# Sketched attention and a four-expert layer: keys issued ahead of the sketch matrices, pieces dealt to other slots, and a tail of 384 columns in two stores

## The chip, the cores and the metric

The kernel runs on one core of a Trainium2 chip. The metric is device time in microseconds (us). The core's engines have each their own instruction stream: TensorE (PE in the profile; PEld is its weight load), VectorE (DVE), ScalarE (ACT), GpSimd (POOL), and SyncE (SP), which here only issues DMAs. They wait for one another by semaphores. SBUF is the on-chip memory, PSUM the eight banks that TensorE writes its sums to.

## The reference

Attention with a quadratic feature map goes ahead of a weighted sum of four two-layer networks:

```python
def phi(x):                                   # 8 x 8 products of two sketches
    a = np.einsum('rd,bhsd->bhsr', S1, x)
    b = np.einsum('rd,bhsd->bhsr', S2, x)
    return np.einsum('bhsi,bhsj->bhsij', a, b).reshape(*x.shape[:-1], r * r)
q_p, k_p = (phi(q), phi(k))
kv = np.einsum('bhsf,bhsd->bhfd', k_p, v)
z = np.sum(k_p, axis=2)
num = np.einsum('bhsf,bhfd->bhsd', q_p, kv)
den = np.einsum('bhsf,bhf->bhs', q_p, z)[..., None] + 1e-06
...
x = attn_out.transpose(0, 2, 1, 3).reshape(B * S, H * D)      # 4352 tokens x 128
p = domain_probs / (domain_probs.sum(-1, keepdims=True) + 1e-09)
for e in range(E):
    h = np.maximum(x @ w1[e], 0.0)
    out += p[:, e:e + 1] * (h @ w2[e])
```

There are 4 batches, 4 heads, 1088 positions, 32 dimensions, sketches of rank 8; 4 experts of 1024 hidden units. All of it is float32. S1 and S2 come as 64-bit floats.

## The kernel before, in words

**Start.** ScalarE issues the load of S1 and SP that of S2, 8 rows each; then SP issues k of batch 0 (`load_k(0)`, 128 rows of 4352 B), the first q, v, and the weights. VectorE turns the 64-bit words of S1 and S2 into floats (`words`, L301 to L327); ScalarE and GpSimd lay them out as the weights sk, sp and sr (L336 to L343). Meanwhile TensorE runs 11 matmuls on constants (`keep_warm`, L275). VectorE transposes k (L424), and the first products k times sk (L287, the helper `on_side`) follow. L456 copies the products out of PSUM, L481 multiplies them into features.

**Columns.** The 4352 tokens are columns, cut into ten chunks: 128, 448, six of 512, 352, 352. For each chunk and each expert there are eight blocks of 128 hidden units. The list of *slots* is chunk by chunk, expert by expert, block by block; the host loop walks through it and writes out every engine's order by hand. One slot does, in this order: `opening` (first matmuls of block i), `second` (second-layer matmuls of block i - 5), `settle`, `third` (last first-layer matmul of earlier blocks, and what makes their parts), `pay` (late passes), and `work`, which deals pieces of attention.

**A block.** Float32 precision is had from fp32r matmuls by splitting operands in parts. First layer: L1068 and L1069 (wa by xa, wb by xb), then ScalarE scales the sum in its bank (L1070, factor 1 + 2^-12), and one slot later L1085 adds wd by xd. The result is split in three:

- ha, by ScalarE (L1103) or VectorE (L1107);
- hb = relu - ha, by VectorE (L1110), which also reads the bank;
- hc: a scaled part by ScalarE (L1105) or POOL (L1119, from ha), then POOL subtracts it from hb (L1120).

Which engine does what is a letter for each block, the *maker*: A has ha and the scaled part on ScalarE, P has ha on ScalarE and the scaled part on POOL, D has ha on VectorE and the scaled part on ScalarE, V makes hc on VectorE (L1112). X is a plain block: ScalarE's relu (L1095) of the whole sum, multiplied in one float32 pass. ha, hb and hc rotate through 5, 5 and 13 tiles; the tiles of hc also serve plain blocks and sums in order. A tile is free again once the matmul that reads it is done. Second layer: L1164 (va by ha) and L1165 (vb by hb) into one of two banks, in turn by expert, and the late passes L1199 (vd by hc, and the plain block), dealt by `DEALT` over the next expert's slots. Then `gather` multiplies by the expert's gate (L1302) and adds to the chunk's total (L1303), on VectorE; the bank is then free for the expert after the next. In chunk 0 the slots are pairs of blocks; the first two experts of chunk 1 are done in whole float32 (L1061, and L1148 for the second layer).

**Weights and tokens.** The parts of w1 (`weight_parts`; L846 scales on ScalarE or, in `split`, L848 on POOL; L851 joins on VectorE) and of w2 (va, vb, vd; L862) are made in slots listed in `W1_AT` and `W2_AT`. The tile of vd lies over the raw w2 and that of va over the raw w1. `token_parts` makes the three parts of a chunk (L851 on VectorE, then L915 on the engine that `XD_BY` names for that chunk).

**Attention in pieces.** `front` yields the attention of batches 1 to 3 as a stream of pieces: the keys of a batch (transposes L424; `key_project_wide`; L476 adds, the products L490 on VectorE, `value_copy` on the engine that `VALUES_BY` names, L434 to L439), and units of queries (transposes L594, products L783 on the engine that `Q_BY` names, stores L761 and re-loads through DRAM, `attend`). How fast pieces are dealt follows from `needed`, the count of pieces by which a chunk must be ready, plus `LEAD`; `FETCH` is the number of pieces between a unit's load and its product, `TOKENS_AT` the slot of chunk 1's token parts, `TURN` the slots between a chunk's last gather and its output transposes. Two clocks that add up what VectorE and ScalarE were given put pieces off, within limits.

**Tail.** The last expert of the last chunk has makers of its own, `MAKER_TAIL`. Its two Y blocks are relu times gate in one VectorE operation each (L1090), written with columns re-ordered by token. `gather_first` (L1291, L1292) gates and adds the early sums of that expert; its late passes go to another bank a (L1202), gated (L1234) and added into a column order by token (L1236). `last_rows` then multiplies the Y blocks with their weights so that tokens come out on partitions (L1247, three groups for 352 columns: 121, 121, 110 partitions) and adds the sums by a unit matrix (L1249); three copies (L1252 VectorE, L1254 ScalarE) and three stores (L1259: SP, ScalarE, and SP again) end the kernel. `ps_a` is one bank, `ps_h` five, `ps_o` two.

Of the kernel before, what the change touches and what calls it, by code (L numbers as in the profile page):

```python
# [24 lines left out]
def kernel(  # L25
# [39 lines left out]
    GE = 160  # L65
    LAG = 5
    GATES = 3
    BUFFERS = (5, 5, 13)
    HA, HB, HC = BUFFERS
    WHOLE = 2  # L70
    TURN = 3
    MAKER = 'VPXPAAAA'
    LATE = 2
    LATER = 99
    MAKER_1 = 'PPXPPDAP'
    MAKER_LATE = 'APXAPADA'
    TAIL = 4
    MAKER_TAIL = "PAVVXXYY"
    LAG_TAIL = 4
    MAKER_END = "PAXPAPAA"  # L80
    DEALT_TAIL = (1, 2)
    DEALT = (0, 1, 1, 2, 2, 2)
    LIMIT = 2000.0
    LIMIT_A = 1e9
    SLOT_A = 1500.0
    SLOT = 1600.0
    PLAIN = (2,)
    FIRST = min(set(range(8)) - set(PLAIN))
# [70 lines left out]
    def xpieces(name, t):  # L159
        return mpool.tile([P, 3, CW], t, tag="x", name=name)  # L160

    s_raw = cpool.tile([R2, 2 * D], I32, name="s_raw")
    for i, (eng, src) in enumerate(((nc.scalar, S1), (nc.sync, S2))):
        eng.dma_start(s_raw[R * i : R * i + R, :], src.bitcast(I32))

# [29 lines left out]
        i, c = divmod(P * b, HF)  # L195
        return of[e][i][:, c : c + P]

    load_k(0)
    sr = xpieces("sr", F32)
    qn[0] = mpool.tile([P, 3, CW], F32, tag="x", name="qn_first").rearrange("p i c -> p (i c)")[:, 0:S]  # L200
    load_rows(q, 0, qn[0], slice(0, P))
# [72 lines left out]
            wp = psum(ps_h, "h")  # L274
            nc.tensor.matmul(wp[:, :], warm[:, 0:P], warm[:, :], start=True, stop=True)  # L275
# [804 lines left out]
    def third(upto):  # L1080

        while begun and begun[0][0] < upto:
            i, g, w, x = begun.pop(0)
            _, m, e, b = slots[i]
            nc.tensor.matmul(g, w, x, start=False, stop=True, skip_group_check=True)  # L1085
            n = g.shape[-1]
            if plain_block(m, e, b):
                hid[i] = plain_tile()[:, 0:n]
                if maker(m, e, b) == "Y":
                    nc.vector.scalar_tensor_tensor(  # L1090
                        out=by_token(hid[i], n), in0=by_block(g, n), scalar=0.0,
                        in1=by_block(gate[m, e], n), op0=ALU.max, op1=ALU.mult,
                    )
# [12 lines left out]
            if by in "DQ":  # L1106
                nc.vector.tensor_scalar(out=ha, in0=g, scalar1=0.0, scalar2=NEAR, op0=ALU.max, op1=ALU.mult)  # L1107
            if by == "S":
                nc.scalar.activation(hc, high, ACTF.Copy, scale=R12)
            nc.vector.scalar_tensor_tensor(out=hb, in0=g, scalar=0.0, in1=high, op0=ALU.max, op1=ALU.subtract)  # L1110
            if by == "V":
                nc.vector.scalar_tensor_tensor(out=hc, in0=high, scalar=-R12, in1=rest, op0=ALU.mult, op1=ALU.add)  # L1112
            elif by == "N":
                whole = apool.tile([P, CW], F32, tag="fs", name="hs")[:, 0:n]
                nc.scalar.activation(whole, high, ACTF.Copy, scale=1.0 + R12)
                nc.vector.scalar_tensor_tensor(out=hc, in0=g, scalar=0.0, in1=whole, op0=ALU.max, op1=ALU.subtract)
            else:
                if by in "PQ":
                    nc.gpsimd.tensor_scalar(out=hc, in0=high, scalar1=R12, scalar2=1.0, op0=ALU.mult, op1=ALU.mult)  # L1119
                nc.gpsimd.tensor_tensor(out=hc, in0=rest, in1=both_, op=ALU.subtract)  # L1120
            hid[i] = ha, hb, hc
# [3 lines left out]
    def second(i):  # L1125
# [3 lines left out]
        if k == 0:  # L1129
            later = []  # L1130
            acc[m, e] = [None, later]
        if k == (FIRST if kind == "one" else 0):
            acc[m, e][0] = bank(m, e)
        o, later = acc[m, e]
        if kind == "pair":
# [15 lines left out]
        elif kind == "one":  # L1151
            w = slice(DM * k, DM * (k + 1))
            va, vb, vd = w2_parts[e]
            last = max(b for b in range(FB) if not plain_block(m, e, b))
            if plain_block(m, e, k):
                at = DM * (FB - 1 - k)
                rows = w2_tail[:, at : at + DM] if final(m, e) else w2_plain[:, e, 0:DM]
                if maker(m, e, k) == "Y":
                    weighted.append((rows, hd))
                else:  # L1160
                    later.insert(len(later) if final(m, e) else 0, (rows, hd))
            else:
                ha, hb, hc = hd
                nc.tensor.matmul(o[:, 0:n], va[:, w], ha, start=(k == FIRST), stop=False)  # L1164
                nc.tensor.matmul(o[:, 0:n], vb[:, w], hb, start=False, stop=(k == last))  # L1165
                later.append((vd[:, w], hc))
            if final(m, e):
                if k == last:
                    gather_first(m, e, o[:, 0:n])
                    owed.append([0, m, e, psum(ps_a, "a")[:, 0:n], later, DEALT_TAIL])  # L1170
            elif k == FB - 1:
                if O_BY[e] == "A":
                    nc.scalar.activation(o[:, 0:n], o[:, 0:n], ACTF.Copy, scale=1.0 + R12)
                else:
                    nc.vector.tensor_scalar(
                        out=o[:, 0:n], in0=o[:, 0:n], scalar1=1.0 + R12, scalar2=1.0, op0=ALU.mult, op1=ALU.mult
                    )
                owed.append([0, m, e, o[:, 0:n], later, DEALT])
# [9 lines left out]
    def pay():  # L1188

        for r in list(owed):  # L1190
# [5 lines left out]
            for _ in range(min(count, len(passes))):  # L1196
# [40 lines left out]

    def last_rows(m):

        n, t = CHUNKS[m], ordered[0]  # L1240
        u = n // 32
        cuts = [(c, min(c + P // u * u, n)) for c in range(0, n, P // u * u)]
        banks = [psum(ps_h, "h") for _ in cuts]
        rows_of = []
        for k, (rows, h) in enumerate(weighted):
            for r, (c, d) in zip(banks, cuts):
                nc.tensor.matmul(r[0 : d - c, 0:DM], h[:, c:d], rows, start=(k == 0), stop=False)  # L1247
        for x, (r, (c, d)) in enumerate(zip(banks, cuts)):
            nc.tensor.matmul(r[0 : d - c, 0:DM], t[:, c:d], unit[:, 0:P], start=False, stop=True)  # L1249
            ob = mpool.tile([P, CW], F32, tag="hb", bufs=HB, name="ob")[0 : d - c, 0:DM]  # L1250
            if x == 1:
                nc.vector.tensor_copy(ob, r[0 : d - c, 0:DM])  # L1252
            else:
                nc.scalar.copy(ob, r[0 : d - c, 0:DM])  # L1254
            rows_of.append((c, d, ob))
        for x in (0, 2, 1):
            c, d, ob = rows_of[x]
            at = (START[m] - S * (B - 1)) // 32 + c // u * G
            (nc.scalar if x == 1 else nc.sync).dma_start(  # L1259
                bass.AP(out.tensor, out.offset + ((B - 1) * S + at) * DM, [[G * DM, (d - c) // u], [1, u * DM]]),  # L1260
                ob,
            )

    def turn_back(m, src):
# [207 lines left out]
```

## Time and profile before

| what | value |
|---|---|
| runs shown | 454.05, 454.16, 455.1 us |
| median | 454.16 us |
| profiled execution | 453.98 us; its span 452.2 us |
| granted clock of TensorE | 1.000 |
| ScalarE's first issue (S1), from the span's start | 0.74 us |
| last store landed | 451.23 us |
| bytes moved | 34.53 MB, 75 GB/s of HBM over the span |

The span reaches from the first to the last instruction; the execution's time is 1.8 us longer. A row of groups gives the line, engine, operation, output and input tiles with their shapes, the count, then the busy time and the mean of one. The costliest groups besides matmuls:

```profile
L1120 POOL TENSOR_TENSOR hc<-hb,hc 128x512 fp32r<-128x512 f32 (+2 forms) x233 | 282.7, 1234 | 27.7 <-DVE hb L1110 16.6
L1110 DVE SCALAR_TENSOR_TENSOR hb<-h,ha 128x512 fp32r<-128x512 f32 (+2 forms) x235 | 150.6, 646 | 106.6 <-ACT hc L1105 35.3
L1070 ACT ACTIVATE h<-h 128x512 f32<-128x512 f32 (+2 forms) x272 | 154.0, 566 | 10.0 <-PE h L1069 7.5
```

The last column is the time for which the engine stood idle ahead of such an instruction, and what ended most of that wait.

### The profile page before, as it was taken

To read this page: it belongs to the slowest core of one execution; us is meant where nothing else is said; L and a number is where in the kernel's file an instruction comes from. 1 tells how busy PE (TensorE), PEld (TensorE's weight loads), DVE (VectorE), ACT (ScalarE), POOL (GpSimd) and SP (SyncE) were. 2 spreads that over 40 slices of the span, in tenths; PEclk is the share of its full clock that TensorE was granted. 3 is DMA by queue.
4 is the path that set the end of the run, shared out by engine and by line. 5 is a ranking of instruction groups with operands and counts; after the bars stand their busy time and mean duration, and the time that the engine had idled before them with its cause. 6 is when DMAs were issued, how large, how long until landed. Compare 5 with 4: busy or idle time off the path is not lost.

```text
span 452.2 us, 8686 instructions
## 1 busy us (share of the span) xinstructions
PE 442.0 (98%) x2780; PEld 349.1 (77%) x2780; DVE 317.7 (70%) x570; ACT 385.9 (85%) x810; POOL 368.1 (81%) x393
## 2 busy tenths in 40 slices
PE   9999999999999998999999999999999999999995
PEld 6875577877777775777777787777777778999995
DVE  6979879476866759575867659476666667666664
ACT  4377687899999896898989989798989899999991
POOL 6312349999999987898999879998999988899990
PEclk9999999999999999999999999999999999999999
DMA  8906130543332231434412230313313220021100
GB/s 241 312 12 164 45 95 2 108 96 82 120 87 58 41 91 23 121 68 103 150 37 76 48 84 23 101 55 76 80 58 77 45 60 22 18 63 44 34 17 17
DMA packets 49406, 34.53 MB, mean 76 GB/s; under 512 B 25456, under 2 KB 43856, under 8 KB 49360
## 3 DMA queue, kind: packets, MB, share of 16 engines
q1 hardware_dynamic: 49212, 33.91, 29.2%
q8 instruction: 22, 0.36, 0.3%
q14 instruction: 24, 0.20, 0.2%
q10 hardware_dynamic: 148, 0.06, 0.1%
HBM read 28.81 MB, written 5.15 MB: 75 GB/s over the span
## 4 chain that ended last, share of the span: by engine, by line
PE 88%; DVE 8%; issue 1%; ACT 1%; DMA 0%; POOL 0%; DVEq 0%; ACTq 0%
PE o L1199 16%; PE h L1068 13%; PE h L1085 12%; PE h L1069 12%; PE o L1164 11%; PE o L1165 10%; PE a L287 3%; PE h L1061 3%; PE o L1148 3%; PE h L287 3%; DVE kp L490 2%; DVE hb L1110 1%; PE o L287 1%; PE a L466 1%; PE h L466 1%
## 5 line engine op out<-in xcount | busy, mean ns | idle before, releaser
L1120 POOL TENSOR_TENSOR hc<-hb,hc 128x512 fp32r<-128x512 f32 (+2 forms) x233 | 282.7, 1234 | 27.7 <-DVE hb L1110 16.6
L1110 DVE SCALAR_TENSOR_TENSOR hb<-h,ha 128x512 fp32r<-128x512 f32 (+2 forms) x235 | 150.6, 646 | 106.6 <-ACT hc L1105 35.3
L1070 ACT ACTIVATE h<-h 128x512 f32<-128x512 f32 (+2 forms) x272 | 154.0, 566 | 10.0 <-PE h L1069 7.5
L1103 ACT ACTIVATE ha<-h 128x512 fp32r<-128x512 f32 (+2 forms) x202 | 115.0, 569 | 8.6 <-PE h L1085 3.2
L1068 PE MATMUL h<-xs,wa 128*128 128x512 f32 (+2 forms) x272 | 115.5, 425 | 0.1
L1085 PE MATMUL h<-xs,wd 128*128 128x512 f32 (+2 forms) x272 | 104.7, 385 | 0.7 <-ACT h L1070 0.7
L1069 PE MATMUL h<-xs,wb 128*128 128x512 f32 (+2 forms) x272 | 102.2, 376 | 0.0
L1105 ACT ACTIVATE hc<-h 128x512 fp32r<-128x512 f32 (+2 forms) x160 | 90.8, 567 | 0.1
L1164 PE MATMUL o<-ha,va 128*128 128x512 f32 (+2 forms) x235 | 89.1, 379 | 1.8 <-DVE total L1303 1.7
L1165 PE MATMUL o<-hb,vb 128*128 128x512 f32 (+2 forms) x235 | 87.7, 373 | 0.0
L1199 PE MATMUL o<-hc,vd 128*128 128x512 f32 (+2 forms) x231 | 71.0, 378 | 0.0
L1068 PEld LDWEIGHTS h<-xs,wa 128*128 128x128 f32 x272 | 51.1, 188 | 16.4 <-issue 7.6
L1069 PEld LDWEIGHTS h<-xs,wb 128*128 128x128 f32 x272 | 51.2, 188 | 14.0 <-issue 5.5
L1085 PEld LDWEIGHTS h<-xs,wd 128*128 128x128 f32 x272 | 51.1, 188 | 11.9 <-ACT h L1070 1.7
L1119 POOL TENSOR_SCALAR hc<-ha 128x512 fp32r<-128x512 f32 (+2 forms) x73 | 46.0, 631 | 13.0 <-ACT ha L1103 7.0
L1164 PEld LDWEIGHTS o<-ha,va 128*128 128x128 f32 x235 | 44.1, 188 | 10.3 <-DVE total L1303 2.9
L1165 PEld LDWEIGHTS o<-hb,vb 128*128 128x128 f32 x235 | 44.0, 187 | 7.4
L1199 PEld LDWEIGHTS o<-hc,vd 128*128 128x128 f32 x231 | 42.7, 188 | 7.6
L1199 PE MATMUL o<-hid,w_plain 128*128 128x512 f32 (+2 forms) x66 | 31.8, 563 | 0.0
L1107 DVE TENSOR_SCALAR ha<-h 128x512 fp32r<-128x512 f32 (+2 forms) x33 | 21.3, 646 | 6.3 <-ACT hc L1105 6.3
L1095 ACT ACTIVATE hid<-h 128x512 f32<-128x512 f32 (+2 forms) x35 | 19.6, 561 | 0.4
L915 POOL TENSOR_TENSOR xs<-xs 128x512 fp32r<-128x512 f32 (+2 forms) x7 | 9.2, 1309 | 11.5 <-DVE xs L851 11.5
(167 smaller groups left out, 445.8 us busy)
## 6 DMA issues: line engine op xcount, KB each, us to landing
w_sb<-in_moe_w_dram SPq DMA_DIRECT2D x8, 512.0 KB
gate<-gates SPq DMA_DIRECT2D x16, 256.0 KB
kn<-in_k_dram SPq DMA_DIRECT2D x4, 544.0 KB
vn<-in_v_dram SPq DMA_DIRECT2D x16, 128.0 KB
gate<-gates SPq DMA_DIRECT2D x8, 224.0 KB
qn<-in_q_dram SPq DMA_DIRECT2D x3, 544.0 KB
qs<-rows SPq DMA_DIRECT2D x6, 256.0 KB
qs<-rows SPq DMA_DIRECT2D x12, 128.0 KB
```

The lines of the kernel that those rows point to most:

```text
L1068: nc.tensor.matmul(g, wa[:, e, w], xa, start=True, stop=False)
L1069: nc.tensor.matmul(g, wb[:, e, w], xb, start=False, stop=True)
L1070: nc.scalar.activation(g, g, ACTF.Copy, scale=1.0 + R12)
L1085: nc.tensor.matmul(g, w, x, start=False, stop=True, skip_group_check=True)
L1103: nc.scalar.activation(ha, g, ACTF.Relu, scale=NEAR)
L1105: nc.scalar.activation(hc, g, ACTF.Relu, scale=NEAR * R12)
L1110: nc.vector.scalar_tensor_tensor(out=hb, in0=g, scalar=0.0, in1=high, op0=ALU.max, op1=ALU.subtract)
L1119: nc.gpsimd.tensor_scalar(out=hc, in0=high, scalar1=R12, scalar2=1.0, op0=ALU.mult, op1=ALU.mult)
L1120: nc.gpsimd.tensor_tensor(out=hc, in0=rest, in1=both_, op=ALU.subtract)
L1164: nc.tensor.matmul(o[:, 0:n], va[:, w], ha, start=(k == FIRST), stop=False)
L1165: nc.tensor.matmul(o[:, 0:n], vb[:, w], hb, start=False, stop=(k == last))
L1199: nc.tensor.matmul(o, w, h, start=False, stop=True, skip_group_check=True)
```

## The change

- `load_k(0)` stands ahead of the loads of S1 and S2, and both of these are issued by ScalarE; `keep_warm` issues 10 matmuls, not 11.
- The last two chunks have 320 and 384 columns, not 352 each.
- In the last expert the two Y blocks become T blocks: ScalarE writes relu to an SBUF tile, GpSimd multiplies it by the gate into the order by token. With 384 columns, three groups of 128 give every one of 128 partitions three tokens that lie side by side in the output; the three copies go side by side to one tile of 384 columns, and two stores of 64 partitions each (1536 B a partition) follow, on SP and ScalarE. `DEALT_TAIL` is (2, 2).
- ha has 6 tiles and hc 12.
- Makers: the first of chunk 1's (`MAKER_1`) has two D blocks and ends in A; in chunks from 2 on, block 3 of expert 2 is P instead of A (`MAKER_LATE` is now a tuple by expert). `MAKER`, for chunk 0 alone, serves no block that has a maker.
- `XD_BY`: chunk 7's L915 on VectorE, chunk 8's on POOL. `Q_BY`: two products of batch 2 on POOL. `VALUES_BY`: batch 1's copies on POOL. `W2_BY`: one of expert 2's scalings on POOL.
- `LEAD` 4, `FETCH` 6, `TOKENS_AT` 19, `TURN` 2, and slots in `W1_AT` and `W2_AT`, move pieces by slots.
- `first_of` takes the place of the constant `FIRST`; the makers N, W and Z are used by no block.

```diff
-    BUFFERS = (5, 5, 13)
+    BUFFERS = (6, 5, 12)
-    TURN = 3
-    MAKER = 'VPXPAAAA'
+    TURN = 2
+    MAKER = 'VPXAAPAA'
-    MAKER_1 = 'PPXPPDAP'
-    MAKER_LATE = 'APXAPADA'
+    MAKER_1 = 'PPXPPDDA'
+    MAKER_LATE = ('APXAPADA', 'APXAPADA', 'APXPPADA', 'APXAPADA')
-    MAKER_TAIL = "PAVVXXYY"
+    MAKER_TAIL = "PAVVXXTT"
-    DEALT_TAIL = (1, 2)
+    DEALT_TAIL = (2, 2)
-    TOKENS_AT = 20
+    TOKENS_AT = 19
-    LEAD = 6
+    LEAD = 4
-    XD_BY = 'VPPVPPPPVP'
-    Q_BY = 'VPVPVPVPVPVPVPVPVP'
+    XD_BY = 'PPPVPPPVPP'
+    Q_BY = 'VPVPVPVPPPPPVPVPVP'
-    FETCH = 4
+    FETCH = 6
-    W1_AT = ((2, 5), (3, 14), (0, 14), (1, 14))
-    W2_AT = ((3, 21), (0, 22), (2, 28), (1, 31))
+    W1_AT = ((2, 5), (3, 14), (1, 17), (0, 14))
+    W2_AT = ((3, 17), (0, 22), (2, 28), (1, 32))
-    W2_BY = ('AAPV', 'AAVV', 'AAVV', 'AAPV')
-    VALUES_BY = 'APP'
+    W2_BY = ('AAPV', 'AAVV', 'APVV', 'AAPV')
+    VALUES_BY = 'PPP'
-    CHUNKS = [P, 448] + [512] * 6 + [352, 352]
+    CHUNKS = [P, 448] + [512] * 6 + [320, 384]
...
+    load_k(0)
-    for i, (eng, src) in enumerate(((nc.scalar, S1), (nc.sync, S2))):
-        eng.dma_start(s_raw[R * i : R * i + R, :], src.bitcast(I32))
+    for i, src in enumerate((S1, S2)):
+        nc.scalar.dma_start(s_raw[R * i : R * i + R, :], src.bitcast(I32))
...
-    load_k(0)
-    keep_warm(11)
+    keep_warm(10)
...
+                elif maker(m, e, b) == "T":
+                    above = plain_tile()
+                    nc.scalar.activation(above[:, 0:n], g, ACTF.Relu)
+                    nc.gpsimd.tensor_tensor(
+                        out=by_token(hid[i], n), in0=by_block(above, n), in1=by_block(gate[m, e], n), op=ALU.mult
+                    )
...
     def by_token(t, n):
-        return t[:, 0:n].rearrange("p (w u) -> p u w", w=32)
+        return t[:, 0:n].rearrange("p (j w g) -> p g j w", w=32, g=P // 32)
     def by_block(t, n):
-        return t[:, 0:n].rearrange("p (u w) -> p u w", w=32)
+        return t[:, 0:n].rearrange("p (g j w) -> p g j w", w=32, g=P // 32)
...
-        n, t = CHUNKS[m], ordered[0]
-        u = n // 32
-        cuts = [(c, min(c + P // u * u, n)) for c in range(0, n, P // u * u)]
-        banks = [psum(ps_h, "h") for _ in cuts]
+        t, u, some = ordered[0], CHUNKS[m] // 32, CHUNKS[m] // P
+        cuts = [slice(P * j, P * j + P) for j in range(some)]
+        banks = [psum(ps_h, "h")[:, 0:DM] for _ in cuts]
...
+        ob = mpool.tile([P, CW], F32, tag="hb", bufs=HB, name="ob")
+        for j, (r, c) in enumerate(zip(banks, cuts)):
+            nc.tensor.matmul(r, t[:, c], unit[:, 0:P], start=False, stop=True)
+            if j == 1:
+                nc.vector.tensor_copy(ob[:, c], r)
             else:
-                nc.scalar.copy(ob, r[0 : d - c, 0:DM])
-            rows_of.append((c, d, ob))
-        for x in (0, 2, 1):
-            c, d, ob = rows_of[x]
-            at = (START[m] - S * (B - 1)) // 32 + c // u * G
-            (nc.scalar if x == 1 else nc.sync).dma_start(
-                bass.AP(out.tensor, out.offset + ((B - 1) * S + at) * DM, [[G * DM, (d - c) // u], [1, u * DM]]),
-                ob,
+                nc.scalar.copy(ob[:, c], r)
+        at = START[m] - S * (B - 1)
+        for i, eng in enumerate((nc.sync, nc.scalar)):
+            eng.dma_start(
+                bass.AP(out.tensor, out.offset + ((B - 1) * S + at // 32 + 16 * i * G) * DM, [[G * DM, 16], [1, u * DM]]),
+                ob[HP * i : HP * i + HP, 0 : some * DM],
             )
```

More of the change, by code (lines that the diff above doesn't have):

```diff
@@ L87 @@
     PLAIN = (2,)
-    FIRST = min(set(range(8)) - set(PLAIN))
-    TOKENS_AT = 20
+    TOKENS_AT = 19
     AHEAD = 12
     TOKENS = 6
-    LEAD = 6
+    LEAD = 4
     SETTLE = 1
     SPREAD = 0
-    XD_BY = 'VPPVPPPPVP'
-    Q_BY = 'VPVPVPVPVPVPVPVPVP'
+    XD_BY = 'PPPVPPPVPP'
+    Q_BY = 'VPVPVPVPPPPPVPVPVP'
     O_BY = 'AAAA'
-    FETCH = 4
+    FETCH = 6
     DELAY = 0
-    W1_AT = ((2, 5), (3, 14), (0, 14), (1, 14))
-    W2_AT = ((3, 21), (0, 22), (2, 28), (1, 31))
+    W1_AT = ((2, 5), (3, 14), (1, 17), (0, 14))
+    W2_AT = ((3, 17), (0, 22), (2, 28), (1, 32))
     W1_BY = ('AVV', 'AVV', 'PVV', 'AVV')
-    W2_BY = ('AAPV', 'AAVV', 'AAVV', 'AAPV')
-    VALUES_BY = 'APP'
+    W2_BY = ('AAPV', 'AAVV', 'APVV', 'AAPV')
+    VALUES_BY = 'PPP'
     KEYS_BY = "AAA"
@@ L1029, in maker, with first_of @@
     def maker(m, e, b):
-        return (MAKER_TAIL if final(m, e) else MAKER_1 if m == 1 else MAKER if m < LATE else MAKER_LATE if m < LATER else MAKER_END)[b]
+        return (MAKER_TAIL if final(m, e) else MAKER_1 if m == 1 else MAKER if m < LATE else MAKER_LATE[e] if m < LATER else MAKER_END)[b]
     def plain_block(m, e, b):
-        return maker(m, e, b) in "XY"
+        return maker(m, e, b) in "XYT"
+    def first_of(m, e):
+        return min(b for b in range(FB) if not plain_block(m, e, b))
     def opening(i):
@@ L1112, in third @@
                 nc.vector.scalar_tensor_tensor(out=hc, in0=high, scalar=-R12, in1=rest, op0=ALU.mult, op1=ALU.add)
-            elif by == "N":
-                whole = apool.tile([P, CW], F32, tag="fs", name="hs")[:, 0:n]
-                nc.scalar.activation(whole, high, ACTF.Copy, scale=1.0 + R12)
+            elif by in "NWZ":
+                whole = plain_tile()[:, 0:n]
+                if by == "N":
+                    nc.scalar.activation(whole, high, ACTF.Copy, scale=1.0 + R12)
+                elif by == "Z":
+                    nc.vector.scalar_tensor_tensor(
+                        out=whole, in0=high, scalar=1.0 + R12, in1=g, op0=ALU.mult, op1=ALU.bypass
+                    )
+                else:
+                    nc.gpsimd.tensor_scalar(
+                        out=whole, in0=high, scalar1=1.0 + R12, scalar2=1.0, op0=ALU.mult, op1=ALU.mult
+                    )
                 nc.vector.scalar_tensor_tensor(out=hc, in0=g, scalar=0.0, in1=whole, op0=ALU.max, op1=ALU.subtract)
@@ L1131, in second @@
             acc[m, e] = [None, later]
-        if k == (FIRST if kind == "one" else 0):
+        if k == (first_of(m, e) if kind == "one" else 0):
             acc[m, e][0] = bank(m, e)
@@ L1157, in second @@
                 rows = w2_tail[:, at : at + DM] if final(m, e) else w2_plain[:, e, 0:DM]
-                if maker(m, e, k) == "Y":
+                if maker(m, e, k) in "YT":
                     weighted.append((rows, hd))
@@ L1163, in second @@
                 ha, hb, hc = hd
-                nc.tensor.matmul(o[:, 0:n], va[:, w], ha, start=(k == FIRST), stop=False)
+                nc.tensor.matmul(o[:, 0:n], va[:, w], ha, start=(k == first_of(m, e)), stop=False)
                 nc.tensor.matmul(o[:, 0:n], vb[:, w], hb, start=False, stop=(k == last))
@@ L1202, in pay @@
                 nc.tensor.matmul(o, w, h, start=(len(opened) == 1), stop=True, skip_group_check=True)
-                if len(opened) == FB - MAKER_TAIL.count("Y"):
+                if len(opened) == FB - MAKER_TAIL.count("Y") - MAKER_TAIL.count("T"):
                     last_sums(m, e, o)
@@ L1238, in last_rows @@
     def last_rows(m):
-        n, t = CHUNKS[m], ordered[0]
-        u = n // 32
-        cuts = [(c, min(c + P // u * u, n)) for c in range(0, n, P // u * u)]
-        banks = [psum(ps_h, "h") for _ in cuts]
-        rows_of = []
-        for k, (rows, h) in enumerate(weighted):
[L1246 to L1252, printed above, removed]
-            else:
-                nc.scalar.copy(ob, r[0 : d - c, 0:DM])
-            rows_of.append((c, d, ob))
-        for x in (0, 2, 1):
-            c, d, ob = rows_of[x]
-            at = (START[m] - S * (B - 1)) // 32 + c // u * G
-            (nc.scalar if x == 1 else nc.sync).dma_start(
-                bass.AP(out.tensor, out.offset + ((B - 1) * S + at) * DM, [[G * DM, (d - c) // u], [1, u * DM]]),
-                ob,
+        t, u, some = ordered[0], CHUNKS[m] // 32, CHUNKS[m] // P
+        cuts = [slice(P * j, P * j + P) for j in range(some)]
+        banks = [psum(ps_h, "h")[:, 0:DM] for _ in cuts]
+        for k, (rows, h) in enumerate(weighted):
+            for r, c in zip(banks, cuts):
+                nc.tensor.matmul(r, h[:, c], rows, start=(k == 0), stop=False)
+        ob = mpool.tile([P, CW], F32, tag="hb", bufs=HB, name="ob")
[3 more added lines that the diff above has]
+                nc.vector.tensor_copy(ob[:, c], r)
+            else:
+                nc.scalar.copy(ob[:, c], r)
[4 more added lines that the diff above has]
+                ob[HP * i : HP * i + HP, 0 : some * DM],
             )
```

## The prediction

> **What bounds the kernel.** I read the page first, then TensorE's waits, then each wait in the timeline of the engine it names, and last the windows and the start and end of the span. Line numbers are those of the kernel before.
>
> ```profile
> PE 442.0 (98%) x2780; PEld 349.1 (77%) x2780; DVE 317.7 (70%) x570; ACT 385.9 (85%) x810; POOL 368.1 (81%) x393
> PE 88%; DVE 8%; issue 1%; ACT 1%; DMA 0%; POOL 0%; DVEq 0%; ACTq 0%
> ```
>
> TensorE is busy 442.0 of 452.2 us at a granted clock of 1.0, and 88% of the chain is its own work. The change leaves that work alone: the pass counts stay, and columns cost it linearly (one fp32r pass after the other, start to start: 232 ns at 512 columns, 162 at 352, so 8 + 0.4375 a column; 320 + 384 costs 148 + 176 = 324 = 2 x 162). So time can only come from where TensorE waits, and from both ends. The waits:
>
> ```profile
> PE o L1164 <- DVE total L1303: 1.7, 1, 1.7
> PE h L287 <- DVE qT L594: 0.5, 1, 0.5
> PE h L1249 <- DVE hid L1236: 0.3, 1, 0.3
> PE h L287 <- POOL sr L343: 0.3, 1, 0.3
> ```
>
> The view shows only gaps without a running matmul. Comparing each start-to-start step with its length above gives about 17.6 us of lost time: 4.2 up to 30 us, 1.4 at 62-66, 1.87 at 171-172, 1.1 at 177-182, the rest in crumbs.
>
> **1. The start: k ahead of S.** The first key product L287 starts at 5.75 and reads two things: sk, made of S by VectorE's words chain (S landed 2.29, sk written 4.51), and the first transpose of k:
>
> ```profile
> 0.74 1.54 DMA s_raw<-in_S_dram
> 5.19 1.36 DVE L424 STREAM_TRANSPOSE kp<-kn 128x256 f32<-128x256 f32 x3 [1.22 <-DMA kn<-in_k_dram]
> 0.77 4.70 PE L275 MATMUL h<-const-bfloat16-1.0 128*128 128x512 bf16 x11 [0.77 <-PEq L1456]
> ```
>
> The bracket shows VectorE idle 1.22 us until k landed (5.16). SP issued S2 at 0.74 and k only at 1.20, so k gains 0.46. The later loads on SP gain the same, and one warm-up matmul of 0.43 less keeps the last from ending behind the new start. But S1 and S2 now both stand on ScalarE's queue. The first issue took 0.59, so S2 is 0.59 later: 2.88. Its packets then meet those of k (from 2.21, now 1.75; 0.17 each in the steady part, 0.53 at first): one packet's wait gives 3.05 to 3.4. From S to sk it is 2.22, so L287 is even with before at a landing of 3.48. The table load on ScalarE, pushed back 0.59, ended at 2.65 and stays ahead of sk. I take -0.30 (the steady packet), bounds -0.46 and +0.8 (S2 behind all of k, rival 3).
>
> [...]
>
> **2. The second half of the first large chunk, 60 to 80 us.** VectorE stood 2.58 us before L862 (vd, whose tile overlays weights that the last plain pass L1148 still read). Then came L862, L476, L862 and only then the gather L1302, L1303, whose bank the next L1164 waits for. In the changed instruction order the gather stands directly behind the first vd; the second vd (0.86 from start to start) comes behind an hb. One of two copies that vd_2 waited for goes from ScalarE (va at 54.48, 1.12 of waiting) to POOL (2 x 0.62), and the values' copies of this batch (0.75, 0.75, 0.29) go there too. Against it: two blocks of this chunk have ha made by VectorE (L1107) instead of one, for four passes in this stretch 0.61 each instead of two, +1.2 us, hidden only while VectorE waits anyway. TensorE's loss here, 1.4 + 0.4 + 0.2 through 80 us, shrinks by about the 0.86 less that 0.2 of new work that shows: -0.7, bounds -1.5 (nearly all the loss) and +1.0 (the added VectorE work uncovered).
>
> **3. The keys of batch 2, 168 to 182 us.** The largest single wait:
>
> ```profile
> 169.04 2.92 DVE L490 TENSOR_TENSOR kp<-fs 128x512 f32<-128x512 f32 x1
> 171.88 0.69 DVE L1302 TENSOR_TENSOR o<-o,gate 128x512 f32<-128x512 f32 x1
> 172.60 0.69 DVE L1303 TENSOR_TENSOR total<-o,total 128x512 f32<-128x512 f32 x1
> ```
>
> ```profile
> 168.85 2.56 POOL L1120 TENSOR_TENSOR hc<-hb,hc 128x512 fp32r<-128x512 f32 x2
> ```
>
> ```profile
> 173.34 0.50 PE L1164 MATMUL o<-ha,va 128*128 128x512 f32 x1 [1.70 <-DVE total L1303]
> ```
>
> A key product L490 that takes 0.68 elsewhere took 2.92 beside two POOL subtractions, and the gather stood behind it. Its siblings took 0.81 to 1.93, and L851, also with two SBUF inputs, took 0.61 start to start with POOL idle (30-37 us) and up to 1.75 beside L862. With the pieces one to two slots elsewhere (LEAD, FETCH, TOKENS_AT), the changed order at batch 2 reads L1110 x3, L490, L1302, L1303, one L490 ahead of the gather: word for word the order that batch 3 has before. There the L490 in that place took 1.33 and TensorE lost 0.39 instead of 1.87, and 0.12 instead of 1.1 at the query turn. So -1.5 from the gather and, of the 1.0, 0.3, since there the turns' place depends on loads too: -1.8. Bounds: -2.6 (both as in batch 3 in full) and 0 (the new neighbour is as bad).
>
> [...]
>
> **4. The balance of makers, chunks and buffers.** In the stages between, little is free:
>
> ```profile
> 340.00:351.30 11.30, 11.30 (x49) 8.81 (x48) 7.16 (x12) 10.95 (x22) 10.93 (x10) 1.00 0.30 73
> 390.00:438.00 48.00, 48.00 (x286) 46.41 (x285) 31.52 (x63) 47.66 (x128) 45.23 (x56) 1.00 0.18 41
> ```
>
> (Columns: length, then busy TensorE, its loads, VectorE, ScalarE, POOL.) TensorE loses nothing there, yet ScalarE is at 47.66 of 48. Block 3 of expert 2 goes from maker A to P: a 0.48 write less for ScalarE, a 0.63 scaling more for POOL, whose 512-column expert goes from 7 x 1.252 + 2 x 0.63 = 10.02 to 10.65 of TensorE's 11.3. Two query products (1.26 and 0.45) come to POOL in batch 2, and the chunk-7 sum L915 goes to VectorE (1.49 to 1.64 there) while that of chunk 8 comes back. At 320 columns ScalarE has 7.10 of 7.19 by the linear rows, at 384 8.22 of 8.56. With 12 instead of 13 hc buffers a write waits for a pass one matmul (0.23) later; most of these follow a 0.49 ha write on ScalarE, which covers it. All this is under the bound, and the twelve hc tiles let POOL fall behind by some blocks before anyone waits: I take +0.4 (the VectorE sum, 0.2, and one hc wait), bounds 0 and +6.3 (rival 2).
>
> **5. The end.** VectorE works through from 442.4 to 447.0, and then come the stores:
>
> ```profile
> 443.37 1.42 DVE L1090 SCALAR_TENSOR_TENSOR hid<-h,gate 128x352 f32<-128x352 f32 x2
> 446.25 0.77 DVE L1236 TENSOR_TENSOR hid<-a,total 128x352 f32<-128x352 f32 x1
> 447.07 0.92 PE L1249 MATMUL h<-unit,hid 128*121 128x128 f32 x6 [0.35 <-DVE hid L1236]
> 447.94 1.85 SPq L1259 DMA_DIRECT2D out_dram<-ob  x2
> 448.20 0.95 ACTq L1259 DMA_DIRECT2D out_dram<-ob  x1
> ```
>
> The two L1090 leave VectorE (-1.42) for ScalarE (two Relu of about 0.50) and POOL (two multiplies of 384 columns, 0.97 at its linear rate, up to 1.5 each if the strided write costs what it costs VectorE: L1236 0.77 against 0.53). POOL's last operation ended at 441.16, so it is free, and its second multiply would end at 445.2 to 446.1. VectorE is no longer late but the last pass into bank a is (445.4): from there L1234 and L1236 at 384 columns, 0.56 + 0.84, end at about 446.83 (before 447.02): -0.19. The stores: three issues of 0.91, 0.95 and 0.83, the third behind the first on SP, landed 450.24, 450.70 and 451.23. Two stores of 64 partitions start together when the last copy ends (448.2), take 0.5 to 0.6 to issue as L761's 64 rows do, and land 1.4 to 1.55 behind that: 450.1 to 450.4, -0.9 all told. Bounds: -1.2 and +0.8 (rival 4).
>
> **Sum.** -0.3 - 0.7 - 1.8 + 0.4 - 0.9 = -3.3 on the profiled execution's 453.98 (span 452.2 and 1.8 around it), so 450.7. The median shown, 454.16, lies 0.18 above that execution.
>
> **The rivals.**
> 1. The stall stays: the L490 ahead of the gather meets two subtractions again. For it: the spread of its siblings, 0.68 to 2.92. Against: only one of eleven was that long. Term 3 becomes 0: 452.5.
> 2. Slower: POOL becomes the bound. Place: expert 2 of the six 512 chunks and the two last, 0.63 a time on a POOL already busy 10.93 of 11.3 at 340-351. It decides once the backlog passes what the following expert (1.28 spare) pays back and the five hb buffers are held, some 3 us; then all that POOL gets shows: 8 x 0.63 = 5.0 and 1.7 of query products, less the 0.4 by which its chunk sums shrink (512 to 320 columns): 6.3 for term 4's 0.4, so 456.6. Against: the spare of its neighbours is twice the surplus.
> 3. S2 drains behind all of k: it lands near 4.3 (k's last packet 4.09), L287 at 6.55, +0.8 for -0.3: 451.8.
> 4. POOL's strided multiplies take over 2 us each: the second ends at 447.1, behind L1236, and the end is +0.8 for -0.9: 452.4. For it: that write shape is nowhere on POOL before. Against: 1.5 is the dearest ratio seen.
>
> **Chances.** My forecast 0.52, rival 1 0.15, rival 2 0.08, rival 3 0.12, rival 4 0.13. A difference under 0.3% (1.36 us: 452.8 to 455.5) cannot be told from none. Of the forecast 0.03 lies within that, of rival 1 0.05, rival 2 0.02, rival 3 0.01, rival 4 0.04; slower is 0.06 of rival 2. So faster 0.79, same 0.15, slower 0.06. The range reaches up to rivals 1 and 4 with a stray of 1.1, and down to the terms 2, 3 and 5 at two thirds of their better bounds: 449.2 to 453.6.
>
> **What would show it.** L424 at about 4.75 and L287 before 5.5 (term 1); a gather that starts before 64 us (2); no wait over 0.5 at batch 2's L1302 (3); windows between 100 and 438 us with TensorE still full (4); POOL's last multiply ended before L1236 starts, and both stores landed by 450.5 on this clock less the earlier gains (5). A L915 on VectorE that ends ahead of a gather, or hb waiting for POOL in a row, would prove me wrong.

## The result, and the profile after

The changed kernel takes 457.27 us (median of six runs, 455.77 to 458.29) against 454.34 for the kernel before: a ratio of 1.0061, 95% interval 1.004 to 1.0083. It is **slower by about 2.9 us**, where I had forecast 3.3 us faster; the range ended at 453.6. The profiled execution took 458.15 us (span 456.4). Its lines are numbered by the changed file: L286 is L287 of before, L335 is L336, L398 is L399, L475 is L476, L489 is L490, L782 is L783, L1070 is L1068, L1118 is L1110, L1137 is L1120, L1315 and L1316 are L1302 and L1303.

The page's totals say little: TensorE's work is the same.

```profile
PE 443.1 (97%) x2779; PEld 350.0 (77%) x2779; DVE 316.5 (69%) x568; ACT 380.2 (83%) x799; POOL 378.0 (83%) x408
PE 72%; DMA 4%; DVE 2%; POOL 1%; issue 1%; SPq 1%; ACT 0%; DVEq 0%; ACTq 0%; POOLq 0%
```

What is new is that DMA has 4% of the chain where it had 0%. TensorE's waits name the places (total, times, longest, in us):

```profile
PE h L286 <- ACT sk L335: 2.6, 1, 2.6
PE h L1070 <- DVE hb L1118: 1.3, 1, 1.3
PE a L465 <- DVE fs L475: 0.9, 1, 0.9
```

The 1.7 us wait for the gather is gone, as forecast; three others are there instead. The best view of where time goes is the start of the same matmul in both kernels. The last first-layer pass of a block (wd by xd, L1085 before) is counted from 0 to 271; the table gives each kernel's start less that of before (profiled executions, us):

| milestone | before, at | changed | a_start | a_gate | a_start_gate | b_start | b_tail |
|---|---|---|---|---|---|---|---|
| first key product | 5.78 | +1.37 | +0.22 | +1.15 | +0.25 | +1.33 | +0.15 |
| block 0 | 55.91 | +2.92 | +0.24 | +2.70 | +0.30 | +2.95 | +0.37 |
| block 32 | 105.56 | +5.56 | +2.87 | +3.27 | +0.88 | +2.66 | +0.40 |
| block 64 | 153.36 | +5.56 | +2.88 | +3.28 | +0.89 | +2.66 | +0.40 |
| block 96 | 208.86 | +3.08 | +0.41 | +0.80 | -1.59 | +2.66 | -2.27 |
| block 271 | 442.80 | +3.80 | +1.09 | +1.88 | -1.08 | +2.74 | -1.54 |
| end of span | 452.18 | +4.18 | +0.53 | +1.33 | -1.61 | +2.71 | -2.04 |

The kernels that keep the start of before begin the first key product anywhere from 5.78 us (before) to 6.23 (b_tail_one), so a difference under about 0.4 between two columns is not read as an effect. The column of the changed kernel has the whole story: +2.9 before the first block, +2.6 at 60 to 105 us, -2.5 in the keys of batch 2, +0.7 in the late chunks, +0.4 at the end.

**The start.** S2's eight packets moved at 3.68 to 3.86 us, where k's 128 rows (1.77 to 4.04) ran out: 125 of them had started ahead of S2's first packet. Before, S had been through at 1.80. The timeline of VectorE, then of TensorE (start, us, engine, line, operation, idle before and releaser):

```profile
4.85 0.34 DVE L300 TENSOR_SCALAR words<-s_raw 16x32 int32<-16x32 int32 x3 [3.94 <-DMA s_raw<-in_S_dram]
```

```profile
7.14 3.17 PE L286 MATMUL h<-sk,kp 128*64 128x64 f32 x55 [2.57 <-ACT sk L335]
```

VectorE waited 3.94 us for S. The transposes of k stand behind the words of S in its order and began only at 6.44, so that k was of no use without S. And behind the pause TensorE ran at half its clock. The windows (length, then busy PE, PEld, VectorE, ScalarE, POOL, then the granted clock, DMA share, GB/s):

```profile
7.20:10.60 3.40, 3.40 (x66) 3.40 (x68) 1.62 (x5) 1.19 (x4) 1.91 (x6) 0.50 1.05 347
10.60:14.00 3.40, 3.40 (x101) 3.40 (x100) 2.50 (x10) 1.88 (x6) 2.14 (x9) 1.00 1.06 331
```

Both rows are full of TensorE work; the column with 0.50 is what tells them apart, and a busy share would never have shown it.

**60 to 105 us.** The query rows of batch 1 came 9 us late. SP's waits, then VectorE's timeline:

```profile
SPq L398 <- DVE o L1315: 22.3, 1, 22.3
```

```profile
98.25 1.68 DVE L782 TENSOR_TENSOR qs<-qs 128x512 f32<-128x512 f32 x1 [2.10 <-DMA qs<-rows]
99.86 1.27 DVE L1118 SCALAR_TENSOR_TENSOR hb<-h,ha 128x512 fp32r<-128x512 f32 x2
```

SP's timeline, changed:

```profile
88.73 1.16 SPq L760 DMA_DIRECT2D rows<-qT  x2
```

and before:

```profile
79.85 1.17 SPq L761 DMA_DIRECT2D rows<-qT  x2
```

A gate load (L398) stood on SP for 22.3 us, until a gather that began at 87.71 gave its tile free. The query rows' store is the next thing in SP's stream: it went out at 88.73 instead of 79.85, the re-load landed at 98.2, and VectorE's product waited for it with the hb of the next blocks behind it. TensorE lost 1.6 us at 98 and 0.5 at 102. The other 0.6 of the 2.6 lies before block 24, at the wait of 0.9 for L475.

### The profile page after: what moved, and what is told of

It is laid out like the page before. It is cut to its first block, busy times and chain, and to the rows that moved or that the text cites. A ratio compares the mean times of both kernels' runs of the same rounds, so it can differ in the third digit from the quotient of the medians.

```text
span 456.4 us, 8713 instructions
## 1 busy us (share of the span) xinstructions
PE 443.1 (97%) x2779; PEld 350.0 (77%) x2779; DVE 316.5 (69%) x568; ACT 380.2 (83%) x799; POOL 378.0 (83%) x408
## 4 chain that ended last, share of the span: by engine, by line
PE 72%; DMA 4%; DVE 2%; POOL 1%; issue 1%; SPq 1%; ACT 0%; DVEq 0%; ACTq 0%; POOLq 0%
PE o L1216 15%; PE h L1070 11%; PE h L1087 11%; PE h L1071 10%; PE o L1181 10%; PE o L1182 9%; PE a L286 2%; DMA qs<-rows 2%; PE h L286 1%; POOL hc L1137 1%; DMA xd<-y 1%; DMA ring<-xd 1%; PE a L465 0%; DMA rows<-qT 0%; DVE total L1316 0%
## 5 line engine op out<-in xcount | busy, mean ns | idle before, releaser
L1137 POOL TENSOR_TENSOR hc<-hb,hc 128x512 fp32r<-128x512 f32 (+3 forms) x233 | 281.4, 1227 | 23.1 <-DVE hb L1118 10.3
L1118 DVE SCALAR_TENSOR_TENSOR hb<-h,ha 128x512 fp32r<-128x512 f32 (+3 forms) x235 | 150.7, 644 | 109.7 <-ACT hc L1113 40.6
L1072 ACT ACTIVATE h<-h 128x512 f32<-128x512 f32 (+3 forms) x272 | 154.9, 570 | 14.8 <-PE h L1071 13.2
L1111 ACT ACTIVATE ha<-h 128x512 fp32r<-128x512 f32 (+3 forms) x200 | 114.3, 572 | 6.9 <-PE h L1087 0.9
L1070 PE MATMUL h<-xs,wa 128*128 128x512 f32 (+3 forms) x272 | 116.7, 429 | 1.3 <-DVE hb L1118 1.3
L1087 PE MATMUL h<-xs,wd 128*128 128x512 f32 (+3 forms) x272 | 104.5, 384 | 0.4 <-ACT h L1072 0.4
L1071 PE MATMUL h<-xs,wb 128*128 128x512 f32 (+3 forms) x272 | 102.1, 375 | 0.0
L1181 PE MATMUL o<-ha,va 128*128 128x512 f32 (+3 forms) x235 | 89.1, 379 | 0.5 <-DVE total L1316 0.2
L1113 ACT ACTIVATE hc<-h 128x512 fp32r<-128x512 f32 (+3 forms) x154 | 87.5, 568 | 0.3 <-PE o L1216 0.2
L1182 PE MATMUL o<-hb,vb 128*128 128x512 f32 (+3 forms) x235 | 87.7, 373 | 0.0
L1070 PEld LDWEIGHTS h<-xs,wa 128*128 128x128 f32 x272 | 51.1, 188 | 18.6 <-issue 8.0
```

The source lines that it names most:

```text
L1070: nc.tensor.matmul(g, wa[:, e, w], xa, start=True, stop=False)
L1071: nc.tensor.matmul(g, wb[:, e, w], xb, start=False, stop=True)
L1072: nc.scalar.activation(g, g, ACTF.Copy, scale=1.0 + R12)
L1181: nc.tensor.matmul(o[:, 0:n], va[:, w], ha, start=(k == first_of(m, e)), stop=False)
```

## The experiments

All times of this section are medians of several runs. Each ratio is to runs of the kernel before that were measured beside them (medians 454.1 to 454.35).

**a_start: the start undone.**

```diff
-    load_k(0)
-    for i, src in enumerate((S1, S2)):
-        nc.scalar.dma_start(s_raw[R * i : R * i + R, :], src.bitcast(I32))
+    for i, (eng, src) in enumerate(((nc.scalar, S1), (nc.sync, S2))):
+        eng.dma_start(s_raw[R * i : R * i + R, :], src.bitcast(I32))
...
+    load_k(0)
...
-    keep_warm(10)
+    keep_warm(11)
```

> The changed kernel with the start of before alone: S1 on ScalarE and S2 on SP ahead of k, 11 warm-up matmuls. Theory: S2's packets stand behind all of k's (3.68 us instead of 1.70), sk is written at 7.05 instead of 4.51, TensorE pauses 2.57 us and is then granted 0.5 of its clock for 3.41 us. The first fully split block ran 2.9 us later than before; undoing the start should give back 2.9 in the profile (from 458.15 to about 455.2), L286 at 5.75, a clock of 1.0 from the start, and runs as close together as those of before (a spread under 1 us, where the changed kernel has 2.5). Rival: the time to 30 us is set by later loads, which come 0.46 earlier in the changed kernel, so under 1.5 us comes back: 456.7.

Measured: 454.60 us, ratio to before 0.9999 (0.9991 to 1.0008). Block 0 comes back from +2.92 to +0.24, and the median by 2.67: the theory's size. The earlier later loads were worth nothing. The runs still spread 2.1 us, so that part of the expectation fails.

**a_warm: six more warm-up matmuls in the pause.**

```diff
-    keep_warm(10)
+    keep_warm(16)
```

> The changed kernel with 16 warm-up matmuls instead of 10, so that TensorE works until sk is there (the last ends at about 7.13) while S stays late. Theory (a pause of 2.6 us costs the clock): the clock stays 1.0 and the 1.7 us of half speed go, 1.3 of lateness stays: about 456.4 in the profile, and the spread of the runs shrinks. Rival (the clock falls by what kind of work TensorE does, not by the pause): the slice at 7 to 10.6 us still shows 0.5 and the time stays at 458. The instruction fetch of 16 KB that ran from 452.8 to 454.1 beside the last stores of the changed kernel should come a little earlier, as TensorE's stream is 6 matmuls longer; if it is over before 453.3 the last landing is at most 454.2 less the gain, another 0.8 us.

Measured: 456.03 us, ratio 1.0039 (1.0024 to 1.0055). S is as late, L286 starts at 7.26, but the clock holds (same windows as above):

```profile
7.20:10.60 3.40, 3.34 (x95) 3.37 (x97) 2.34 (x9) 2.52 (x8) 2.41 (x7) 1.00 1.03 341
```

95 matmuls where the changed kernel got through 66, and block 0 is 1.41 us earlier. So of the 2.9 us at the start about 1.4 are the half clock and 1.5 the late S. The warm-ups did not fill the pause: from 3.6 us on each took 0.22 us in place of 0.43, the last ended at 5.75 and not at 7.13, and 1.5 us of idle time were left, which did not cost the clock. The six runs of the changed kernel agree: the two with a mean clock of 0.998 took 455.77 and 456.43, the four with 0.994 to 0.996 took 457.12 to 458.29. The other parts of the expectation fail: the instruction fetch did not come a little earlier but after the stores, and the runs still spread (454.62 to 457.24).

**a_gate: the gate load behind the query rows.**

```diff
-        yield
+        for _ in range(4 if (m, e) == (1, 2) else 1):
+            yield
         next_gates()
```

> The changed kernel with one gate load (issued after the third gather of chunk 1) put 3 slots later in SP's stream, behind the query rows of batch 1. Theory: that load waited 22.3 us on SP for a gate tile, up to 88.4 us, and the query rows' store behind it went out at 88.7 instead of 79.9; the query product on VectorE then waited for them until 98.25, with the hb of the blocks behind it, and TensorE lost 2.5 us at 98 to 103. Without it the rows go out before 84, no wait of TensorE over 0.5 us is left between 95 and 104, and the profile's time falls by about 2.0 to 2.5 (some of it may be hidden behind other waits). Rival: the pieces come too late for another reason (LEAD 4, FETCH 6), the product is as late, and nothing changes (under 0.5 us).

Measured: 456.05 us, ratio 1.0032 (1.0017 to 1.0047). SP issues the rows at 84.61 (82.21 in a_start_gate, whose start is not late), VectorE's wait for them is gone, and block 32 moves from +5.56 to +3.27: 2.3 us. The median moves by only 1.2, in a kernel whose start still scatters.

**a_start_gate: both.**

> Both of these: the start of before, and the gate load later in SP's stream. Theory: 2.9 and 2.2 add up, since they lie 90 us apart: about 453.0 in the profile, 1 us faster than before, with the gain of 2.2 us at batch 2's gather and part of the earlier end kept. Rival: TensorE, no longer late there, runs into the same makers' waits and the sum is under 3 us: 455.

Measured: 452.71 us, ratio 0.9968 (0.9956 to 0.998): 4.6 us under the changed kernel, 1.6 under before, and 1.9 under a_start, where the gate load's share shows without the scatter. The two causes add, and together they are more than the whole loss.

**b_start: the kernel before with the changed start alone.** The edit is a_start's the other way round.

> The kernel before with the changed start alone (k ahead of S, S1 and S2 on ScalarE, 10 warm-up matmuls). Theory (the start alone makes the loss): S2's packets behind k's, at 3.7 us; L287 at about 7.1; in many runs half the clock for 3.4 us behind the pause; the profile 2.9 us (1.3 where the clock stays) over before's, the median of the runs 1.5 to 2.9 over it, with a spread over 2 us. Rival (the start costs only together with the later changes): under 1 us.

Measured: 456.74 us, ratio 1.0055 (1.0037 to 1.0074). Its column in the table is +2.7 from block 32 to the end: nothing after the start gives the time back.

**a_k4: k still ahead of S, in four DMAs** (on a_gate, with 11 warm-ups).

```diff
-    load_k(0)
+    kn[0] = lpool.tile([P, S], F32, tag="rows", name="kn")
+    for i in range(4):
+        nc.sync.dma_start(
+            kn[0][32 * i : 32 * i + 32, :], bass.AP(k.tensor, k.offset + 32 * i * G * D, [[G * D, 32], [1, S]])
+        )
```

> The changed kernel with the moved gate load, and k of the first batch still issued ahead of S, but in four DMAs of 32 rows. [...]

Measured: 453.78 us, ratio 0.9998 (0.9986 to 1.0011). S2's packets moved at 2.66 to 3.01 us while k's ran until 4.30: 56 of k's 128 rows had started ahead of the first and 70 ahead of the last, so they came in between. S2 was issued at 1.39 us, behind two quarters of k (0.74 and 1.21) and ahead of two (1.65 and 2.12), and came through where about two quarters had started; by what rule the queues take turns, the run does not show. The clock stayed at 1.0. But L290 (L286 in the changed kernel) began only at 6.52, against 5.78 before:

```profile
4.22 0.34 DVE L304 TENSOR_SCALAR words<-s_raw 16x32 int32<-16x32 int32 x3 [3.30 <-DMA s_raw<-in_S_dram]
```

From the last packet to VectorE's start 1.2 us went by, against 0.5 before (1.80 to 2.31), where k's first packet began to move at 2.21. The time is 1.4 us over a_start_gate by the ratios, and the start is only 0.5 of that (block 0 at +0.77 against +0.30); another 0.6 comes between blocks 96 and 271, which the start does not explain and no run here settles.

**b_tail: the kernel before with the changed tail alone** (chunks of 320 and 384, T blocks, the order by token, two stores).

```diff
-    MAKER_TAIL = "PAVVXXYY"
-    DEALT_TAIL = (1, 2)
-    CHUNKS = [P, 448] + [512] * 6 + [352, 352]
+    MAKER_TAIL = "PAVVXXTT"
+    DEALT_TAIL = (2, 2)
+    CHUNKS = [P, 448] + [512] * 6 + [320, 384]
...
```

> The kernel before with the changed tail alone: chunks of 320 and 384, T blocks, order by token in groups of 128, two stores of 64 partitions. Theory: from TensorE's last matmul to the end of the span 3.67 instead of 4.19 (as in the changed kernel with the start of before), and VectorE's 1.42 us off the way to the last pass; in all 0.5 to 0.9 us faster than before, 453.5. Rival: chunks of 320 and 384 cost as much in waits of ScalarE and POOL as the tail gives (the kernel with the start of before and the moved gate load lost about 1 us against before between the first block of chunk 8 and the last of chunk 9): no change, 454.3.

Measured: 452.41 us, ratio 0.9959 (0.9945 to 0.9972). Faster than expected, and not at the end: the stall of batch 2 is gone here too (block 96 at -2.27). From TensorE's last matmul to the end it is 3.66 us instead of 4.19, the expected 0.5; and from block 96 to 271 it loses 0.7; the other kernels of the table with these chunks lose 0.5 to 1.1 there, b_start with the old ones 0.1.

**a_keys: another bank for the third key group** (on a_start_gate).

```diff
-            kf.append(psum(ps_h, "h") if gi == 1 else psum(ps_a, "a"))
+            kf.append(psum(ps_h, "h") if gi else psum(ps_a, "a"))
```

> The changed kernel with the start of before and the moved gate load, and the third group of a batch's key products in another PSUM bank, so that it needn't wait for the sum L475 of the first group, which in the changed order stands behind the gather, an hb and the copy of the first. Theory (the gather came earlier, as forecast, but the key sum behind it now holds TensorE): the wait L465 for L475 of 0.9 us goes, and the profile is 0.5 to 0.9 us faster than that kernel, 451.9 against 452.7. Rival: the blocks behind wait for VectorE anyway, and it comes back as another wait before 80 us: no change.

Measured: 453.93 us, ratio 0.9992 (0.9983 to 1.0). The wait of 0.9 is gone, and others of 1.6 for hb (longest 1.1) stand at 60 to 82 us instead: the rival, and about 1.1 us worse by the ratios. That the blocks miss the bank, one of their five, is argued from the edit, not shown.

**b_tail_deal, b_tail_mid, b_tail_bal: one group of edits each, on b_tail.**

```diff
-    TURN = 3
-    LEAD = 6
-    FETCH = 4
+    TURN = 2
+    LEAD = 4
+    FETCH = 6
```

> The kernel before with the changed tail, and LEAD 4, FETCH 6, TURN 2 besides. Theory (the pieces moved by these three are what put a gate load ahead of the query rows of batch 1 on SP): SP waits about 20 us for that gate tile, the rows go out near 88, VectorE's product waits until about 98, and the time is 1.5 to 2.5 us over that of the changed tail alone (452.4): 454.4. Rival: without the other edits the product falls into a gap of VectorE and costs under 0.5 us.

Measured: 456.46 us, ratio 1.0052 (1.0039 to 1.0065), 4.1 over b_tail. The theory's part is there: SP waits 23.3 us for a gate tile, the rows go out at 87.51, and 1.9 us are lost between blocks 24 and 32. Another 2.1 were lost before block 8: the third key group waits 2.02 us for the key sum L476. So the three numbers LEAD, FETCH and TURN hold the second cause; which of them decides was not separated.

```diff
-    MAKER_1 = 'PPXPPDAP'
-    TOKENS_AT = 20
-    W1_AT = ((2, 5), (3, 14), (0, 14), (1, 14))
-    W2_AT = ((3, 21), (0, 22), (2, 28), (1, 31))
-    W2_BY = ('AAPV', 'AAVV', 'AAVV', 'AAPV')
-    VALUES_BY = 'APP'
+    MAKER_1 = 'PPXPPDDA'
+    TOKENS_AT = 19
+    W1_AT = ((2, 5), (3, 14), (1, 17), (0, 14))
+    W2_AT = ((3, 17), (0, 22), (2, 28), (1, 32))
+    W2_BY = ('AAPV', 'AAVV', 'APVV', 'AAPV')
+    VALUES_BY = 'PPP'
```

> The kernel before with the changed tail and the edits of the second part of chunk 1 (MAKER_1, W1_AT, W2_AT, W2_BY, VALUES_BY, TOKENS_AT). My prediction had -0.7 for it. Theory now: the gather there comes earlier, but the key sum L476 behind it holds a PSUM bank that TensorE wants, so nothing is won: 0 to +0.6 over the changed tail alone. Rival (the prediction): 0.4 to 1.0 us faster.

Measured: 454.90 us, ratio 1.0022 (1.0013 to 1.0031), 2.5 over b_tail, which neither expects. At blocks 15 to 64 it is 0.23 *ahead* of b_tail, where I had predicted 0.7 for these edits; but b_tail_one, with b_tail's order on every engine up to the last store, is 0.21 ahead there too, so this is no gain that can be told. The loss lies between blocks 64 and 80, 2.7 us against b_tail: the stall of batch 2 is back. This pair shows it best. VectorE and POOL in b_tail (there L1126 is POOL's subtraction):

```profile
169.44 0.73 DVE L490 TENSOR_TENSOR kp<-fs 128x512 f32<-128x512 f32 x1
```

```profile
168.34 1.29 POOL L1126 TENSOR_TENSOR hc<-hb,hc 128x512 fp32r<-128x512 f32 x1
169.58 0.74 POOL L439 COPY vx<-vn 64x128 f32<-64x128 f32 x1
```

The same in b_tail_mid:

```profile
169.21 2.91 DVE L490 TENSOR_TENSOR kp<-fs 128x512 f32<-128x512 f32 x1
```

```profile
168.78 0.28 POOL L439 COPY vx<-vn 64x128 f32<-64x128 f32 x1
169.03 2.54 POOL L1126 TENSOR_TENSOR hc<-hb,hc 128x512 fp32r<-128x512 f32 x2
171.66 0.95 POOL L1125 TENSOR_SCALAR hc<-ha 128x512 fp32r<-128x512 f32 x1
```

VectorE's stream is L490, hb, hb, L490, gather in both. POOL's is not the same: in b_tail the small copy L439 stands behind a subtraction and ahead of the next two, in b_tail_mid it stands ahead of two subtractions back to back. In b_tail the second L490 starts 0.14 us ahead of the copy and takes 0.73, while the copy takes 0.74 instead of 0.28. In b_tail_mid L490 comes 0.18 us into the first of the two subtractions and ends 0.5 us behind the second: 2.91. The kernel before has b_tail_mid's order there, and both before and b_start show the same picture (0.19 us in, 2.92 and 2.90). So the stall goes with the order in which POOL was given its work; that the two engines wait for each other is argued from these times.

```diff
-    BUFFERS = (5, 5, 13)
-    MAKER_LATE = 'APXAPADA'
-    XD_BY = 'VPPVPPPPVP'
-    Q_BY = 'VPVPVPVPVPVPVPVPVP'
+    BUFFERS = (6, 5, 12)
+    MAKER_LATE = ('APXAPADA', 'APXAPADA', 'APXPPADA', 'APXAPADA')
+    XD_BY = 'PPPVPPPVPP'
+    Q_BY = 'VPVPVPVPPPPPVPVPVP'
```

> The kernel before with the changed tail and the balance edits (tiles 6 and 12, block 3 of expert 2 from A to P, XD_BY, Q_BY); TensorE's order is the same, instruction for instruction. The prediction had 0 to +0.4, its slower rival +6.3. Theory: POOL stays under TensorE's time in every expert, and the time is within 0.5 us of the changed tail alone. Rival (POOL becomes the bound): over 2 us slower, hb waiting for POOL in expert 2 of the 512 chunks.

Measured: 452.34 us, ratio 0.9967 (0.9956 to 0.9977): b_tail's time. POOL is not the bound.

**b_tail_one: a single store** (on b_tail, 128 partitions on SP).

> The kernel before with the changed tail, but with one store of all 128 partitions on SP in place of two of 64 on SP and ScalarE. Theory (two halves side by side save nothing over one, since both use the same DMA engines; what was won came from 16 engines in place of 11, 1536 B rows, and no third store behind the first): within 0.3 us of the two stores, from TensorE's end to the span's end 3.5 to 3.9. Rival (the halves' issues in parallel matter): 0.4 to 0.8 us slower.

Measured: 451.99 us, ratio 0.9954 (0.994 to 0.9967), the fastest of all; from TensorE's end to the end 3.53 us against 3.66. The second half store on ScalarE is worth nothing.

## Why the prediction was wrong

In the profiles the forecast was missed by 7.5 us (4.2 slower, not 3.3 faster): 3.2 in term 1, 2.1 in a step that it did not have, 1.3 each in terms 2 and 5, 0.3 in term 4, less 0.7 by which term 3 gave more.

**Term 1, the start, failed most.** "S2's packets then meet those of k ...: one packet's wait gives 3.05 to 3.4" was the wrong step: S2 waited until nearly all of k had moved (125 of 128 rows). I had that as rival 3, with a chance of 0.12 and a price of +0.8, and both were too small. It cost 2.6 to 2.9 (b_start, a_start). The price missed two things: VectorE could start on S 1.0 us behind the end of its last packet (3.88 to 4.85), not 0.5, and the pause made TensorE run 3.41 us at half clock, 1.4 us that no term had. That one packet's wait would be enough was my estimate, and no run shows it: S2's packets moved from 3.68 us on with k in one load, and from 2.66 on with k in four loads, two of them issued ahead of S2 (a_k4). Why S2 waited so long, no run shows.

**Term 2, the second half of chunk 1, was wrong in its cover.** I predicted -0.7 from a gather that comes earlier. It does come earlier in the order, but alone the edits gave nothing that can be told (b_tail_mid). With LEAD, FETCH and TURN the key sum stands behind the gather and TensorE waits for its bank (0.9, in b_tail_deal 2.0), so that the changed kernel loses 0.6 from block 0 to block 24.

**A step is missing: SP.** I followed every engine whose instructions the change moved, and I said that pieces move "one to two slots", but I did not follow the query rows' store past the gate load in SP's stream. That cost 2.0 to 2.3 us, shown by a_gate and, cleanest, by a_start_gate against a_start. The step could have been had from the changed order alone: it shows two gate loads where there was one ahead of that store, and the second waits for a gather, which ended 8.5 us after the rows' old time.

**Term 3 came out, but not for its reason.** -1.8 predicted; blocks 64 to 96 give -2.5, and the order was as I had read it:

```profile
174.52 1.26 DVE L489 TENSOR_TENSOR kp<-fs 128x512 f32<-128x512 f32 x1
175.70 0.69 DVE L1315 TENSOR_TENSOR o<-o,gate 128x512 f32<-128x512 f32 x1
```

1.26 where batch 3 had 1.33. The reason that I gave was VectorE's order, but b_tail loses the stall with VectorE's order of before (the two are the same up to 193 us) and b_tail_mid has it again. What changes with the stall is POOL's stream (L490 0.73 us in b_tail, 2.91 in b_tail_mid). In the changed kernel POOL has a copy behind the subtraction that L489 meets, and the prediction says nothing of it: the gain is in part luck. Why L490 takes 2.91 beside two subtractions, and why POOL took its second one ahead of the waiting L490, no run shows.

**Term 4 was right in size by luck**, +0.4 against about +0.7 from block 96 to 271. I had taken it for VectorE's sum and a wait for an hc tile, from the balance edits; these add nothing that can be told (b_tail_bal). The loss is there with the changed tail alone (b_tail), where I had put the chunks of 320 and 384 under the bound; whether the chunks or the pieces that move with them make it was not separated. Rival 2, the slower one that I named, did not occur.

**Term 5 was half as large.** Predicted -0.9; the stores give -0.5 (a_start, b_tail). The 0.19 that I had ahead of them did not come: from block 271 to TensorE's last matmul it is 5.2 us in before and in b_tail. The two multiplies on POOL took 1.99 together, as the linear rate said (0.97 each). In the changed kernel's own profile even that is lost:

```profile
446.84 1.99 POOL L1099 TENSOR_TENSOR hid<-hid,gate 128x384 f32<-128x384 f32 x2 [1.07 <-ACT hid L1098]
452.08 0.61 SPq L1272 DMA_DIRECT2D out_dram<-ob  x1
452.08 0.65 ACTq L1272 DMA_DIRECT2D out_dram<-ob  x1
```

Fifteen of each store's sixteen shares were complete by 453.91 and 454.16, the last at 454.73 and 454.98. A fetch of 16 KB of instructions ran on the DMA engines from 452.82 to 454.13; that it held up these two shares is argued from the times, since the trace names no engine. In a_warm, where a fetch of that size came only at 455.47, the 4.61 us from TensorE's last matmul to the end became 3.67; no run moved the fetch alone.

What stays open is the scatter of the kernels with the late S (455.34 to 458.43 for the changed kernel and b_start), which is not the clock alone: b_start's slowest run had a mean clock of 1.0.

## What to carry to other kernels

When a load is moved ahead of a small one, ask which of the two the next step needs last, and price the case in which the small one waits for all of the large one, even if another engine issues it: here S2, issued by ScalarE, came behind 125 of the 128 rows that SP had issued, at 3.68 us. When pieces of work are moved by slots, follow the issuing queue too: here one gate load stood on SP for 22.3 us, and the query rows' store behind it went out at 88.73 us instead of 79.85. And a wait that hangs on what two engines happen to run side by side can go, or come back, with edits made for another reason (L490 took 2.92 us before, 0.73 in b_tail, 2.91 in b_tail_mid); a change that removes it may not have removed its cause.

## What the runs showed of the hardware

- The granted clock was 0.50 for 3.41 us (7.21 to 10.62) behind a pause of TensorE of 2.57 us in the changed kernel, and for 3.42 us (8.37 to 11.79) behind one of 2.0 us in b_start. Behind a pause of 1.5 us it was 1.00 (a_warm, 7.20 to 14.00); a_keys, with a pause of 1.4 us at the start, had a mean clock of 0.999 over its profiled execution.
- VectorE started 0.5 us behind the end of S's last packet where S moved ahead of k's packets (before, first packet of k at 2.21, and a_start), and 0.8 to 1.2 us behind it where packets of k were moving (a_gate 0.8, b_start 0.9, the changed kernel 1.0, a_warm 1.1, a_k4 1.2).
- A key product of VectorE that took 0.73 us beside a small POOL copy (b_tail) took 2.91 where it met two POOL subtractions back to back (b_tail_mid).
